# Forgetting attention and a SiLU layer on one core: v loads held behind the load of f, a weight load issued one step earlier, a larger budget of MoE work

## The chip, the cores and the metric

The kernel runs on one core of a Trainium2 chip. A core has five engines with their own instruction streams: PE (TensorE, matrix multiply), ACT (ScalarE, activations), DVE (VectorE), POOL (GpSimd) and SP (SyncE, which only issues transfers). Sixteen DMA engines serve all transfers of the core. The metric is the device time of one execution in microseconds (us); less is better.

## The reference

Attention over 8 batches and 8 heads, 576 positions, head size 64, with a decay between positions that comes from a gate f; then a two-layer network with a SiLU on the rows of the result. In short:

```python
def _attn_ref(q, k, v, f):                      # q, k, v: (8, 8, 576, 64); f: (8, 8, 576)
    scores = scale * np.matmul(q, k.transpose(0, 1, 3, 2))
    cum = np.cumsum(np.log(np.clip(f, 0.0001, 1.0)), axis=-1)
    decay = cum[:, :, :, None] - cum[:, :, None, :]
    scores = np.where(causal, -1000000000.0, scores + decay)
    attn = np.exp(scores - np.max(scores, axis=-1, keepdims=True))
    attn = attn / (np.sum(attn, axis=-1, keepdims=True) + 1e-09)
    return np.matmul(attn, v)

def _moe_ref(x, w_in, w_out):                   # x: (4608, 512), w_in: (512, 2048), w_out: (2048, 512)
    h = x @ w_in
    return (h * (1.0 / (1.0 + np.exp(-h)))) @ w_out
```

## The kernel before

The order of every engine's instructions is the order in which the program writes them (`manual_schedule`); the only freedom is when each one's waits are over. Waits are derived from the tiles: an instruction that reads a tile waits for who wrote it, and one that overwrites a tile waits for who still reads it, transfers included.

**The gate.** f is loaded by SP into `f_sb` (L206). DVE clips it in place (L236), ACT takes the logarithm in place (`Ln`, L242), and `weights_scan` (L244) makes the cumulative sum on DVE (L245), a mask tile `ban` on DVE (L257), and the exponential `wexp` on ACT (L254). ACT loads a table for each of the two functions. `weights` (L266) transposes `wexp` on PE and copies it to `w_bf`. The decay then needs no add in the scores: the values v, and a column of ones beside them, are multiplied by `w_bf`.

**First blocks.** The first 128 positions of each batch are treated by themselves. `load_qk0` (L128) and `load_v0` (L137) load q, k and v; POOL issues these, except v of batches 0 and 1, which SP issues (L140). `turn0` (L277) transposes q and k on PE, ACT and DVE copying them out of PSUM. `ban0` (L297) puts the mask into the scores' PSUM by a matmul, `scores0` (L309) adds the scores and takes the exponential on ACT. `convert_v0` (L339) multiplies v by the weights on POOL, `out0` (L349) makes the output (L359) and divides it, `back0` (L382) transposes it into a tile x for the network. Batches 0 to 3 come first in the program, then 4 and 5, then 6 and 7 (`two_more`, L805).

**MoE.** `load_w_in` (L188) and `load_w_out` (L192) each load a quarter of a weight matrix, from POOL's queue. The network's first layer is cut into chunks (`m1_chunk`, matmuls at L567: one of 16 slices of the hidden size for one group of rows), the second into parts (`m2_part`, matmuls at L612: four of the 16 slices for 128 rows). A planner puts these between the steps of attention: `fill(us)` (L698) writes as many of them as make up that much modelled PE time, and what is left over or overdrawn is carried to the next `fill`. So a number handed to `fill` decides which PE instructions stand in front of which.

**Rest blocks.** Positions 128 to 575 follow, in a loop over pairs of heads (`for m in range(NQ)`, two pairs at a time). SP loads q, k and v of later pairs, POOL casts q and k (`cast_qk`, L399) and converts v (L413), SP issues a transposing DMA (L427), and PE makes the scores from its result (L459) and the output (L506). SP's loads for this begin behind one small transfer that reads `w_out_bf` and writes a tile nobody uses, so that SP waits there until that weight has landed:

```python
    def after(ap):
        nc.sync.dma_start(out=junk[0:1, 0:16], in_=ap)
```

The program's opening lines, as the change finds them:

```python
    nc.sync.dma_start(out=f_sb[:, :], in_=f.rearrange("b h s -> (b h) s"))
    load_qk0(0)
    load_v0(0)
    load_v0(1)
    ...
    nc.vector.tensor_scalar(
        out=f_sb[:, :], in0=f_sb[:, :], scalar1=1e-4, scalar2=1.0, op0=ALU.max, op1=ALU.min
    )
```

Of the kernel before, what the change touches and what calls it, by code (L numbers as in the profile page):

```python
# [10 lines left out]
FP32 = mybir.dt.float32  # L11
# [7 lines left out]
def kernel(  # L19
# [10 lines left out]
    nc = tc.nc  # L30

    B, H, S, D = q.shape
# [23 lines left out]
    const = ctx.enter_context(tc.tile_pool(name="const", bufs=1))  # L56
# [22 lines left out]
    ban = const.tile([P, NP, P], BF16, name="ban")  # L79
    warm = const.tile([P, SM], BF16, name="warm")  # L80
    junk = const.tile([1, 16], BF16, name="junk")
    kT0 = [const.tile([P, NP, P], BF16, name=f"kT0_{b}") for b in range(B)]
    v0 = [const.tile([P, H, D + 1], BF16, name=f"v0_{b}") for b in range(B)]
    vps = [const.tile([P, NM, H, D + 1], BF16, name=f"vp_{i}") for i in range(2)]
# [43 lines left out]
    def load_qk0(b):  # L128
        t = conv.tile([P, 2, RUN * D], BF16, name="qkb", tag="qkb")
        for i, src in enumerate((q, k)):  # L130
            nc.gpsimd.dma_start(
                out=t[:, i, :],
                in_=src[b, :, 0:P, :].rearrange("h (r c) d -> r h (c d)", c=RUN),
            )
        qk0[b] = t

    def load_v0(b):  # L137
        t = vfs[b % 4]
        q_ = nc.sync if b < 2 else nc.gpsimd
        q_.dma_start(out=t[:, :, 0:D], in_=v[b, :, 0:P, :].rearrange("h p d -> p h d"))  # L140
        vf0[b] = t
# [46 lines left out]
    def load_w_in(i):  # L188
        c0, c1 = i * DFF // WQ, (i + 1) * DFF // WQ
        nc.gpsimd.dma_start(out=w_in_bf[:, :, c0:c1], in_=w_in_v[:, :, c0:c1])  # L190
# [14 lines left out]
    f_sb = setup.tile([BH, S], FP32, name="f_sb")  # L205
    nc.sync.dma_start(out=f_sb[:, :], in_=f.rearrange("b h s -> (b h) s"))  # L206
    load_qk0(0)
    load_v0(0)
    load_v0(1)
    make_identity(nc, ident_bf)  # L210
# [9 lines left out]
    for i in range(2):  # L220
        for g in range(2):
            nc.vector.tensor_copy(
                out=sel[:, i, :].rearrange("p (u w r) -> p u w r", u=2, w=2)[:, g, :, :],
                in_=ident_bf[:, :].rearrange("p (r u i w) -> p u i w r", u=2, i=2, w=2)[
                    :, g, i, :, :
                ],
            )

    def keep_warm(n):
# [7 lines left out]
        out=f_sb[:, :], in0=f_sb[:, :], scalar1=1e-4, scalar2=1.0, op0=ALU.max, op1=ALU.min  # L237
# [39 lines left out]
    def turn0(b, i):  # L277
        src = qk0[b]
        if i == 0:
            qT0[b] = qktp.tile([P, NP, P], BF16, name="qT0", tag="qT0", bufs=2)  # L280
        dst, evac = ((qT0[b], nc.scalar.copy), (kT0[b], nc.vector.tensor_copy))[i]
        tp = pbig.tile([P, NP, NRUN, RUN], FP32, name="tp", tag="big")
        for c in range(RUN):
            for j in range(2):
                nc.tensor.matmul(
                    tp[j * D : (j + 1) * D, :, :, c].rearrange("p a r -> p (a r)"),
                    lhsT=src[:, i, c * D : (c + 1) * D],
                    rhs=sel[:, j, :],
                    start=True,
                    stop=True,  # L290
                )
        evac(
            out=dst[:, :, :].rearrange("p a t -> p (a t)"),
            in_=tp[:, :, :, :].rearrange("p a r c -> p (a r c)"),
        )

    def ban0(b):  # L297
        sc = psc.tile([P, 2, NP, P], FP32, name="sc", tag="sc")
        for i in range(2):
            nc.tensor.matmul(  # L300
                sc[:, i, :, :].rearrange("p a t -> p (a t)"),
                lhsT=ident_bf[:, :],
                rhs=ban[:, :, :].rearrange("p a t -> p (a t)"),
                start=True,
                stop=False,
            )
        return sc

    def scores0(b, sc=None):  # L309
        t = qT0.pop(b)  # L310
        fresh = sc is None
        u = upool.tile([P, 2, NP, P], BF16, name="u", tag="u")
        u0[b] = u
        if fresh:
            sc = psc.tile([P, 2, NP, P], FP32, name="sc", tag="sc")
        for p in range(NP):
            for i in range(2):
                r = slice(i * D, (i + 1) * D)
                nc.tensor.matmul(
                    sc[:, i, p, :],  # L320
                    lhsT=kT0[b][r, p, :],
                    rhs=t[r, p, :],
                    start=fresh,
                    stop=fresh or p == NP - 1,
                )
        nc.scalar.activation(
            out=u[:, :, :, :].rearrange("p i a t -> p (i a t)"),
            in_=sc[:, :, :, :].rearrange("p i a t -> p (i a t)"),
            func=ACT.Exp,
            scale=scale,  # L330
        )
# [7 lines left out]
    def convert_v0(b):  # L339
        nc.gpsimd.tensor_tensor(  # L340
            out=v0[b][:, :, :],
            in0=vf0.pop(b)[:, :, :],
            in1=w_bf[:, 0, b * H : (b + 1) * H, None].to_broadcast([P, H, D + 1]),
            op=ALU.mult,
        )
# [310 lines left out]
    def step(force=0):  # L656

        a, c = at["m1"], at["m2"]
        want = wanted(a, c)
        if not want:  # L660
            return None
        g1 = M1[a][0] if a < len(M1) else NG
        g2 = M2[c][0] if c < len(M2) else NG
        can1 = g1 in ready and not (M1[a][1] == 0 and g1 > g2 + 1)
        can2 = open2["w"] and c < len(M2) and g2 < g1
        kind = force if (force == 1 and can1) or (force == 2 and can2) else want
        if kind == 1:
            if M1[a][1] == 0:
                begin[g1] = (0, c)
            m1_chunk(g1, M1[a][1])  # L670
            at["m1"] += 1
            t = 4 * (GW[g1] / 2.4 + 2.5)
        else:
            m2_part(*M2[c])
            at["m2"] += 1
            t = 4 * (DM / 2.4 + 2.5)
        return t
# [6 lines left out]
    def plan(us_):  # L684

        a, c, kinds = at["m1"], at["m2"], []
        while us_ > 0:
            k = wanted(a, c)
            if not k:
                break  # L690
            kinds.append(k)
            if k == 1 and M1[a][1] == 0:
                begin[M1[a][0]] = (0, c)
            us_ -= (4 * (GW[M1[a][0]] / 2.4 + 2.5) if k == 1 else 4 * (DM / 2.4 + 2.5)) / 1000
            a, c = a + (k == 1), c + (k == 2)
        return kinds

    def fill(us_, least=0, ends=(0, 0)):  # L698

        left = us_ + at["left"]  # L700
        kinds = plan(left)
        kinds += [0] * (least - len(kinds))
        if any(ends) and kinds:
            if 2 not in kinds:
                kinds[0] = 2
            n1, n2 = len(kinds) - kinds.count(2), kinds.count(2)
            e0 = 1 if ends[0] else 0
            e1 = 1 if ends[1] and n2 > e0 else 0
            inner = n2 - e0 - e1
            n = n1 + inner  # L710
            mid = [2 if (x + 1) * inner // n > x * inner // n else 1 for x in range(n)]
            if inner and mid[-1] == 2 and e1 and not e0:
                mid = mid[::-1]
            kinds = [2] * e0 + mid + [2] * e1
        for k in kinds:
            t = step(k)
            if t is None:
                at["left"] = 0.0
                return
            left -= t / 1000  # L720
        at["left"] = left
# [22 lines left out]
    out0(0, apart=True)  # L744
    turn0(3, 0)
    scores0(2, ban0(2))
    convert_v0(2)
    load_w_in(1)
    turn0(3, 1)
    bans = ban0(3)  # L750
    out0(1, apart=True)
# [80 lines left out]
    fill(6.0)  # L832
    two_more(6, False)
    ready.add(2)
    fill(3.2)

# [101 lines left out]
```

## Time and profile before

| what | value |
|---|---|
| device time, median of 3 runs | 344.5 us (344.4 to 344.6) |
| span of the profiled execution | 342.2 us |
| the rest of the median, around that span | 2.3 us |
| PE busy | 334.3 us (98% of the span) |
| ACT, DVE, POOL busy | 216.8, 180.5, 130.0 us |
| DMA engines' mean busy share, 20 to 50 us | 1.15 to 1.21 by ten-microsecond windows |
| last matmul ends | 338.55 us |

The span runs from the first to the last instruction of the program in one profiled execution, and all positions in time are counted from its start; the device time is measured without the profiler, and the table puts their difference down as the rest. [...] PE is busy for nearly the whole span, so what matters is when it is not.

### The profile page before, as it was taken

The numbers are of one execution on the slowest core, as the hardware profiler recorded it, in microseconds if no ns is written. First come the engines' busy times: TensorE is split into PE (matmuls) and PEld (weight loads), VectorE is DVE, ScalarE is ACT, GpSimd is POOL, SyncE is SP. The second block draws the span as 40 slices with busy tenths as digits, with TensorE's granted clock in tenths as the row PEclk, the third lists the DMA queues.
The fourth block names the chain that finished last, engine by engine and source line by source line (L and its number), as shares of the span: only waits on it lengthen the run. The fifth ranks groups of instructions, "written<-read, shape, count | busy, mean of one in ns | idle before, by whom it ended". The sixth has DMA issues, their size and how long they took to land.

```text
span 342.2 us, 8881 instructions
## 1 busy us (share of the span) xinstructions
PE 334.3 (98%) x3560; PEld 198.6 (58%) x3560; DVE 180.5 (53%) x387; ACT 216.8 (63%) x401; POOL 130.0 (38%) x227
## 2 busy tenths in 40 slices
PE   7999999999999999999999999999999999999995
PEld 3645655567656556566465666656656565555654
DVE  4665736357647547357445563655746364444330
ACT  5857645877687676857759677595685944454431
POOL 8895317732618307327325422612830000001011
PEclk9999999999999999999999999999999999999999
DMA  8999999999699889999999789989994010001012
GB/s 154 185 184 221 192 192 155 233 207 190 142 172 205 188 177 168 180 210 156 174 188 188 171 156 202 169 170 165 165 186 101 22 42 33 31 32 61 33 53 72
DMA packets 142457, 50.67 MB, mean 148 GB/s; under 512 B 133328, under 2 KB 139728, under 8 KB 142416
## 3 DMA queue, kind: packets, MB, share of 16 engines
q1 hardware_dynamic: 132400, 32.93, 56.7%
q0 software_dynamic: 9856, 17.04, 21.5%
q8 instruction: 28, 0.46, 0.6%
q10 hardware_dynamic: 160, 0.13, 0.1%
q14 instruction: 13, 0.11, 0.1%
HBM read 36.85 MB, written 9.44 MB: 135 GB/s over the span
## 4 chain that ended last, share of the span: by engine, by line
PE 66%; DMA 14%; SPq 9%; POOL 6%; issue 3%; ACT 0%; POOLq 0%
PE po L612 29%; PE hp L567 25%; DMA vf<-in_v_dram 6%; PE sc L459 5%; SPq L158 5%; PE dn L506 4%; DMA w_out_bf<-in_moe_w_out_dram 3%; PE dn L515 2%; SPq L427 2%; DMA qkT<-qkb 2%; POOL qkb L399 1%; DMA qkb<-in_k_dram 1%; SPq L168 1%; SPq L179 1%; DMA qf<-in_q_dram 1%
## 5 line engine op out<-in xcount | busy, mean ns | idle before, releaser
L576 DVE SCALAR_TENSOR_TENSOR gt<-th,hp 128x384 bf16<-128x384 bf16 (+2 forms) x208 | 105.8, 522 | 119.0 <-ACT th L575 115.5
L575 ACT ACTIVATE th<-hp 128x384 bf16<-128x384 f32 (+2 forms) x208 | 95.2, 478 | 84.3 <-PE hp L567 82.0
L612 PE MATMUL po<-w_out_bf,gt 128*128 128x512 bf16 (+1 forms) x592 | 145.3, 374 | 0.0
L567 PE MATMUL hp<-x,w_in_bf 128*128 128x384 bf16 (+2 forms) x704 | 128.1, 321 | 0.2
L567 PEld LDWEIGHTS <-w_in_bf 128*128 128x128 bf16 x832 | 79.9, 98 | 56.5 <-issue 0.7
L463 ACT ACTIVATE u<-sc 128x1024 bf16<-128x1024 f32 (+1 forms) x96 | 75.3, 822 | 9.5 <-PE sc L459 9.5
L612 PEld LDWEIGHTS <-gt 128*128 128x128 bf16 x592 | 53.3, 98 | 47.9 <-issue 2.5
L591 POOL DMA_DIRECT2D out_dram<-osb x38 | 21.0, 552 | 93.7 <-ACT osb L622 66.7
L413 POOL TENSOR_TENSOR vp<-vf,w_bf 128x520 bf16<-128x520 f32 (+1 forms) x32 | 34.4, 1078 | 41.0 <-DMA vf<-in_v_dram 35.1
L622 ACT ACTIVATE osb<-po 128x512 f32<-128x512 f32 (+1 forms) x37 | 22.1, 597 | 18.9 <-PE po L612 18.9
L399 POOL CAST qkb<-qf 128x384 bf16<-128x384 f32 x32 | 16.7, 521 | 41.9 <-DMA qf<-in_q_dram 41.2
L459 PE MATMUL sc<-qkT 64*128 64x128 bf16 (+1 forms) x640 | 26.9, 207 | 0.9 <-DMA qkT<-qkb 0.8
L459 PEld LDWEIGHTS <-qkT 64*128 64x128 bf16 x640 | 18.4, 94 | 12.5 <-issue 10.2
L467 ACT ACTIVATE ut<-sc 128x640 bf16<-128x640 f32 x32 | 23.3, 729 | 0.0
L476 DVE TENSOR_TENSOR u<-u,tri 128x768 bf16<-128x768 bf16 x32 | 22.1, 690 | 1.2 <-ACT u L463 1.2
L399 POOL CAST qkb<-kf 128x384 bf16<-128x384 f32 x32 | 17.7, 554 | 13.0 <-DMA kf<-in_k_dram 12.8
L506 PEld LDWEIGHTS <-u 128*128 128x128 bf16 x576 | 20.8, 98 | 2.5
L506 PE MATMUL dn<-vp,u 128*128 128x65 bf16 x384 | 21.8, 194 | 0.0
L524 DVE TENSOR_TENSOR xr<-dn,rec 128x448 bf16<-128x448 f32 x32 | 20.0, 624 | 1.1
L506 PE MATMUL dn<-v,u 128*128 128x65 bf16 x192 | 19.8, 194 | 0.0
L482 DVE TENSOR_TENSOR ut<-ut,trit 128x128 bf16<-128x128 bf16 x32 | 11.2, 351 | 15.6 <-ACT ut L467 15.6
L567 PE MATMUL hp<-xt,w_in_bf 128*128 128x256 bf16 x128 | 17.7, 273 | 0.0
(68 smaller groups left out, 203.0 us busy)
## 6 DMA issues: line engine op xcount, KB each, us to landing
out_dram<-osb POOLq DMA_DIRECT2D x32, 256.0 KB, 3.3
vf<-in_v_dram SPq DMA_DIRECT2D x26, 256.0 KB, 4.7
qf<-in_q_dram SPq DMA_DIRECT2D x64, 96.0 KB, 2.9
kf<-in_k_dram SPq DMA_DIRECT2D x64, 96.0 KB, 3.1
w_in_bf<-in_moe_w_in_dram POOLq DMA_DIRECT2D x4, 512.0 KB, 6.9
w_out_bf<-in_moe_w_out_dram POOLq DMA_DIRECT2D x4, 512.0 KB, 9.6
vf<-in_v_dram POOLq DMA_DIRECT2D x6, 256.0 KB, 10.3
qkb<-in_q_dram POOLq DMA_DIRECT2D x8, 128.0 KB, 5.1
```

The costliest lines, as they stand in the source:

```text
L399: nc.gpsimd.tensor_copy(out=t2[:, c0 : c0 + NR, :].rearrange("p c x -> p (c x)"), in_=t[:, :, :, :].rearrange("p c h d -> p (c h d)"),)
L413: nc.gpsimd.tensor_tensor(out=vbf[b][r, c, :, :], in0=vst[b][c][r, :, :], in1=w_bf[r, c + 1, b * H : (b + 1) * H, None].to_broadcast([n, H ...
L459: nc.tensor.matmul(sc[:, i, o : o + q1 - q0], lhsT=kt, rhs=t[r, q0:q1], start=True, stop=True)
L463: nc.scalar.activation(out=u[:, :, c * SM : c * SM + w], in_=sc[:, :, 0:w], func=ACT.Exp, scale=scale)
L467: nc.scalar.activation(out=ut[:, :, 0:3:2, :].rearrange("p k i t -> p i k t"), in_=sc[:, :, T0 : T0 + (NM + 1) * ST].rearrange("p i (k t) ...
L476: nc.vector.tensor_tensor(out=x, in0=x, in1=tri[:, None, None, :].to_broadcast([P, 2, NR, P]), op=ALU.mult)
L506: nc.tensor.matmul(dn[:, i * NR + c - 1, :], lhsT=u[:, i, o : o + P], rhs=vals(kb, i), start=(kb == 0), stop=(kb == c),)
L567: nc.tensor.matmul(hp[:, :], lhsT=w_in_bf[:, cc, fc * P : (fc + 1) * P], rhs=xcols(g, cc), start=(cc == 0), stop=(cc == NCC - 1),)
L575: nc.scalar.activation(out=th[:, :], in_=hp[:, :], func=ACT.Tanh, scale=0.5)
L576: nc.vector.scalar_tensor_tensor(out=gt[:, fc, :], in0=th[:, :], scalar=1.0, in1=hp[:, :], op0=ALU.add, op1=ALU.mult,)
L612: nc.tensor.matmul(po[:, :], lhsT=gt[:, fc, tb * P : (tb + 1) * P], rhs=w_out_bf[:, fc, m0:m1], start=(fc == 0), stop=(fc == NFC - 1),)
L622: nc.scalar.activation(out=osb[:, :], in_=po[:, :], func=ACT.Copy, scale=0.5)
```

## The change

Three edits. SP, after the load of f, gets a transfer of the last 16 numbers of one row of `f_sb` to a new tile that nobody reads; it stands ahead of the two v loads in SP's order. On POOL, the second quarter of w_in is issued ahead of the third conversion of v instead of behind it. And the last `fill` ahead of the rest blocks gets 4.1 instead of 3.2.

```diff
+    junk_f = const.tile([1, 16], FP32, name="junk_f")
...
     nc.sync.dma_start(out=f_sb[:, :], in_=f.rearrange("b h s -> (b h) s"))
     load_qk0(0)
+    nc.sync.dma_start(out=junk_f[0:1, 0:16], in_=f_sb[0:1, S - 16 : S])
     load_v0(0)
     load_v0(1)
     make_identity(nc, ident_bf)
...
     turn0(3, 0)
     scores0(2, ban0(2))
+    load_w_in(1)
     convert_v0(2)
-    load_w_in(1)
     turn0(3, 1)
...
     two_more(6, False)
     ready.add(2)
-    fill(3.2)
+    fill(4.1)
```

## The prediction

> **What bounds the kernel now.** I read the page first, for the engine that carries the span:
>
> ```profile
> span 342.2 us, 8881 instructions
> ...
> PE 334.3 (98%) x3560; PEld 198.6 (58%) x3560; DVE 180.5 (53%) x387; ACT 216.8 (63%) x401; POOL 130.0 (38%) x227
> ```
>
> PE, the matmul engine, is idle for only 7.9 us, of which 3.7 lie behind its last matmul (it ends at 338.55). The change adds and removes no matmul, so it can act on the span only through the other 4.2 us, or by adding idle time. The view of waits, for PE, says where those are:
>
> ```profile
> PE wm L232 <- DVE warm L204: 1.2, 1, 1.2
> PE sc L459 <- DMA qkT<-qkb: 0.8, 2, 0.4
> PE tp L285 <- DMA qkb<-in_q_dram: 0.7, 1, 0.7
> PE tx L389 <- DVE xq L374: 0.5, 1, 0.5
> PE dn L359 <- POOL v L340: 0.4, 1, 0.4
> ```
>
> The 0.8 us at L459 are two waits in the rest blocks, at 74.38 (0.40) and at 111.78 (0.43), where transposed q and k land just too late. Nearly all the rest lies in the first 18 us. So the third view is the timeline of these, all engines (start, duration, engine, line, operation, idle time before it and what ended that):
>
> ```profile
> 0.74 0.59 SPq L206 DMA_DIRECT2D f_sb<-in_f_dram  x1
> 0.74 1.28 ACT L242 ACT_TABLE_LOAD   x1 [0.74 <-PEq L924]
> ...
> 3.63 0.45 DVE L236 TENSOR_SCALAR f_sb<-f_sb 64x576 f32<-64x576 f32 x1
> ...
> 4.11 0.68 ACT L242 ACTIVATE f_sb<-f_sb 64x576 f32<-64x576 f32 x1 [2.09 <-DVE f_sb L236]
> ...
> 6.30 0.29 DVE L257 TENSOR_SCALAR ban<-tri 128x512 bf16<-128x512 bf16 x1
> 6.39 0.78 ACT L254 ACTIVATE wexp<-cum,half 64x576 f32<-64x576 f32 x1 [0.30 <-DVE half L253]
> ...
> 7.16 1.04 PE L300 MATMUL sc<-ban,ident_bf 128*128 128x512 bf16 x4
> ...
> 8.13 0.40 PE L319 MATMUL sc<-qT,kT 64*128 64x128 bf16 x8
> ...
> 9.51 1.05 POOL L340 TENSOR_TENSOR v<-vf,w_bf 128x520 bf16<-128x520 f32 x1 [0.28 <-issue]
> ...
> 16.24 0.42 PE L359 MATMUL dn<-v,u 128*128 128x65 bf16 x8 [0.44 <-POOL v L340]
> ```
>
> The reader is to see one serial chain: f lands at 3.60 (issued 0.74, 2.9 to landing), is clipped in place on DVE, goes through Ln on ACT and the scan on DVE (4.83 to 6.18), then comes ban (which stands behind the scan in DVE's order) and the exponential. PE needs ban at L300, 0.57 us after it is ready (6.59), and the weights shortly after. This chain has half a microsecond of slack, no more.
>
> **Part 1, the hold on v.** SP gets one more DMA, a copy of 64 bytes out of f_sb, ahead of the two v loads. SP waits for f before it issues that copy (3.60), so the v loads go out at about 4.25 and 4.9 instead of 1.39 and 2.0. At 5.4 to 5.9 from issue to landing (v's own rows) they land by 9.7 and 10.8; before, the first was needed at 9.51. Freed of them, the q and k of block 0 should land before the 5.53 and 6.55 of now.
>
> But the copy reads f_sb, and the clip overwrites f_sb in place. In the changed program as built, the clip on DVE waits for two landings, that of f and that of the copy, and ACT's first table load, which now has no wait at all, waits for the copy as well. So the copy's whole trip is added to the chain, and the table load with it, which has been hidden in the wait for f so far (0.74 to 2.02). The sum:
>
> - The copy is issued at 3.62. Its time to landing is not in the trace. The nearest rows are f's own load on the same queue, 2.9 us for 144 KB, and the junk copy of the same form at L200, 5.5 us at 36.46, when the DMA engines are full (share 1.21 in 30 to 40). Taking f's data off (144 KB at about 0.2 MB/us, the rate of the first slices, 0.7 us) leaves 2.2. The copy runs beside the first q and k loads, but with no long queue, so I take 2.5, nearest to f, and keep as ends 5.5 and 1.6 (the 2.2 without the 0.59 that the issue itself takes). It lands at 6.1.
> - ACT's table load then runs from about 6.15 for 1.28; the clip (0.45) lies beside it. Ln starts at 7.45 instead of 4.11: 3.34 later. Scan, half, ban and exponential follow 3.34 later, with nothing else in front of them.
> - PE finishes the transposition of block 0 early (about 6.4) and waits for ban: 6.59 + 3.34 = 9.93. The 0.57 slack is eaten. The scores at L319 also need the copy of q on ACT, which stands behind the exponential (ended 7.64, now 10.98): they start near 11.1 instead of 8.13, 2.95 later. The weights w_bf and POOL's first conversion are late by the same (9.51 becomes 12.45), so the later v costs nothing: the first has landed 2.7 us before.
> - Downstream, 0.35 us come back: the last first-block output (16.24) waited 0.44 for POOL, and without POOL could have started at 15.9, when its exponential was done. POOL's order after 12.45 is conversion, load, conversion, load, conversion, conversion: 4 x 1.05 + 2 x 0.80 = 5.8, so the fourth v is ready at 18.25, and PE is there at 15.9 + 2.95 = 18.85. So MoE work starts 2.6 late, at 20.76 instead of 18.16.
>
> **Part 2, w_in ahead of the third conversion.** Now POOL waits 0.91 for v before that conversion (at 13.30, in the same timeline), and the issue of a load takes 0.80, so the load would be free and the fourth conversion come 0.8 earlier; that is the 0.44 at 16.24. With POOL late by 2.95 the wait is gone anyway, and the issue costs the third conversion 0.8, which is in POOL's sum above and leaves it 0.6 us ahead of PE. The first w_in load moves from 10.51 to about 13.4, its data (5.8 to landing) are there by 19.2, before 20.76. No cost; if that cover were gone, 0.8.
>
> **Part 3, more MoE work in front.** A group of four L567 matmuls of 256 columns takes 0.43 of PE, one of four L612 0.86 (rows of the chain). The built order puts one more L567 group ahead of the first rest score, two by the scores of the fourth head pair, where PE waited 0.40, and one L612 group by the tenth, where it waited 0.43: 0.86 us more work in front of each. After the sixteenth pair it is 0.6 less, since the total is the same. It costs nothing by itself. The loads behind these waits hang on the DMA engines, which are full from 20 to 50 us (share 1.15 to 1.21 by ten-microsecond windows); they are late by what the w_in loads are late, about 1.9: the first lands near 19.2, the second 2.7 behind it (the distance of the third and fourth now, 26.1 and 28.8), at 21.9 instead of 19.99. PE comes 2.6 + 0.86 late. So PE has 1.5 us more distance to its data than now, and both waits, 0.8 together, vanish.
>
> **The sum:** +2.6 - 0.8 = +1.8 on the profiled execution, 342.2 becomes 344.0. The runs' median of 344.5 is 2.3 above that span, and I let that stand: 346.3.
>
> The Trainium skill, page "DMA: Bandwidth & Descriptors", section "Anatomy of one DMA — SWDGE (gpsimd) path", speaks against the added copy: a DMA has a fixed cost of about 2.0 us whatever its size, mostly the receipt of the write. By it the copy would be 2.0 instead of my 2.5 and the sum 345.8; the rows here say 2.9 and 5.5.
>
> **The rivals.** *The hold pays.* If DVE and ACT do not in fact stand behind the copy, q and k come earlier, the scores at L319 start when the unchanged chain allows (7.66 instead of 8.13: 0.47 less), the 0.44 behind POOL goes too, partly the same time (0.55 together), and the two rest waits (0.8): 343.1. The point from which this side decides, where they do stand behind it, is a copy of 0.7: the front loses the copy's time and about 0.1, and the rest blocks give back 0.8. For it: DMA's share in the first 10 us is 0.89, so the loads do collide. Against it: no DMA in the trace lands in under 2.9. Chance 0.05.
>
> *The rest waits stay.* If the loads slip as far as PE does, the 0.8 do not come back: 347.1. The DMA engines are busy without a gap behind the late w_in loads, but the sum there gives them 1.9, less than PE's 2.6. Chance 0.15.
>
> *The clock drops.* PE would idle from about 6.4 to 9.9. The granted clock is 1.00 over the first 112 us and 0.98 over the last 11.2, in which PE stops at 338.55, so some idle time at the end costs it. If the clock were halved for a stretch as long as that gap (3.5 us), PE would lose up to 1.7, and some of that is covered by waits: about 347.6. Chance 0.14.
>
> The Trainium skill, page "TensorE: Matmul & The Clock Gate", Part 1, says that the clock falls to half after an idle window of about 3.4 us that runs freely. By that the gap would be just at the limit, and the dip would come in some executions only.
>
> *The copy is stuck* behind queued packets like the one at 36.46, 5.5 us: 3.0 more, 349.3. Chance 0.06.
>
> **How the numbers follow.** The forecast as summed has the other 0.60. Of it, copies of 1.6 to 3.2 us give 345.4 to 347.0, and a copy of 1.4 or less, which would come within 0.2% (0.7 us, about what a measurement of this kernel can tell from no change), has 0.05. So faster 0.05, same 0.05, slower 0.90. The range 345.4 to 348.2 takes in the forecast, the waits that stay and most of a clock drop; the stuck copy, the hold that pays and the shortest copies, together under 0.2, are left out.
>
> **What would show it.** In the changed profile the clip should start near 6.1 with a DMA as its releaser, the table load near 6.15 instead of 0.74, the first matmul on ban near 9.9 with over 3 us of PE idle time before it, and the first L567 group (L569 there) near 20.8; the waits for qkT at pairs four and ten should be gone. Wrong in the main: a clip that still starts near 3.6. Wrong in size: a copy far from 2.5. Wrong in the middle: waits for qkT that remain while the front is late.

## The result and the profile after

The changed kernel is slower: 349.9 us median (348.1 to 350.8, 6 runs) beside 344.45 for the kernel before in the same series (343.3 to 346.3, 6 runs), a ratio of 1.0159 with a 95% interval of 1.0129 to 1.0188. The sign was forecast, the size was not: +5.5 us where the sum said +1.8, and above the range. Experiments are compared by their ratio to the kernel before, run in the same series, since the runs of one kernel lie 1 to 5 us apart from lowest to highest. Line numbers of the changed kernel are one (up to L207) or two higher than before; kernels with more lines added shift further.

The page of the changed kernel: span, engines, and the granted clock in 40 slices.

```profile
span 348.9 us, 8837 instructions
...
PE 333.0 (95%) x3513; PEld 199.8 (57%) x3560; DVE 179.6 (51%) x387; ACT 216.7 (62%) x401; POOL 129.6 (37%) x227
...
PEclk9699999999999999999999999999999999999999
```

The span is 6.7 longer (this execution took 350.76, a little above its median). PE does no more work; 47 of its 3,560 matmuls are missing from the trace, which is why its sum is even lower. The second digit of the clock is new. Waits of PE (total, number, longest):

```profile
PE sc L302 <- DVE ban L259: 4.2, 1, 4.2
...
PE dn L508 <- DVE gt L578: 1.2, 1, 1.2
PE wm L234 <- DVE warm L205: 1.2, 1, 1.2
PE hp L569 <- DMA x<-xr: 0.5, 1, 0.5
```

The two waits for qkT at L459 (0.8 in all) are gone, as forecast. In their place stand one of 4.2 for `ban`, which was forecast with 3.5, and two that were not: 1.2 at 194.61 and 0.5 at 149.60. The chain that ended last, in order of time (start, duration, what), tells where the 4.2 come from:

```profile
0.75 2.72 DMA f_sb<-in_f_dram
3.46 0.02 issue
3.48 3.78 DMA junk_f<-f_sb
...
7.33 1.28 ACT L244
...
8.63 0.69 ACT f_sb L244
...
9.34 1.36 DVE cum L247
...
10.87 0.21 DVE ban L259
...
11.13 1.87 PE sc L302 x4
12.99 0.54 PE sc L321 x8
```

The copy and ACT's table load now stand in the chain, one behind the other. The copy took 3.78 from issue to landing, not 2.5. And the four matmuls on `ban` took 1.87 where they took 1.04 before: PE was not at full speed. The windows of the changed kernel (PE, PEld, DVE, ACT and POOL busy, then the granted clock, the DMA share and GB/s; the share is the sum of all packets' times over the time of 16 engines, so it can pass 1):

```profile
6.00:9.00 3.00, 0.96 (x21) 0.67 (x18) 0.45 (x1) 1.65 (x2) 3.00 (x9) 0.94 1.16 217
9.00:12.00 3.00, 0.87 (x3) 0.32 (x3) 2.48 (x5) 2.69 (x4) 0.21 (x1) 0.50 1.21 241
12.00:15.00 3.00, 3.00 (x36) 2.04 (x36) 0.49 (x1) 1.18 (x2) 0.26 (x1) 0.50 0.54 120
15.00:18.00 3.00, 2.92 (x82) 2.62 (x80) 1.96 (x5) 2.14 (x3) 2.98 (x4) 0.92 0.21 14
```

The clock was halved from 8.65 to 15.48, two stretches of 3.41 us, although PE's gap was 4.2. One such stretch takes 0.005 off the mean clock of a run, and the six runs have 0.990 (three) and 0.995 (three), so the drop came in all of them, two stretches or one. The DMA share falls to 0.21 in the last window: the first w_in load is issued at 15.74 only, since POOL's first conversion stands ahead of it and waits for the weights. MoE work starts at 23.60 instead of 18.16.

### The profile page after: what moved, and what is told of

The parts are those of the page before. It is cut to its first block, busy times and chain, and to the rows that moved or that the text cites. A ratio compares the mean times of both kernels' runs of the same rounds, so it can differ in the third digit from the quotient of the medians.

```text
span 348.9 us, 8837 instructions
## 1 busy us (share of the span) xinstructions
PE 333.0 (95%) x3513; PEld 199.8 (57%) x3560; DVE 179.6 (51%) x387; ACT 216.7 (62%) x401; POOL 129.6 (37%) x227
## 4 chain that ended last, share of the span: by engine, by line
PE 79%; DMA 7%; SPq 4%; DVE 3%; ACT 3%; issue 3%; POOL 1%; POOLq 0%; ACTq 0%
PE po L614 31%; PE hp L569 31%; PE sc L461 6%; PE dn L508 4%; PE tp L287 2%; PE dn L517 2%; SPq L429 2%; SPq L159 2%; DMA qkT<-qkb 2%; DVE gt L578 1%; DMA x<-xr 1%; DMA vf<-in_v_dram 1%; DMA junk_f<-f_sb 1%; PE sc L302 1%; DMA qf<-in_q_dram 1%
## 5 line engine op out<-in xcount | busy, mean ns | idle before, releaser
L578 DVE SCALAR_TENSOR_TENSOR gt<-th,hp 128x384 bf16<-128x384 bf16 (+2 forms) x208 | 105.4, 522 | 122.1 <-ACT th L577 119.1
L614 PE MATMUL po<-w_out_bf,gt 128*128 128x512 bf16 (+1 forms) x550 | 138.5, 373 | 3.4 <-issue 1.9
L415 POOL TENSOR_TENSOR vp<-vf,w_bf 128x520 bf16<-128x520 f32 (+1 forms) x32 | 35.8, 1124 | 38.3 <-DMA vf<-in_v_dram 27.2
L401 POOL CAST qkb<-kf 128x384 bf16<-128x384 f32 x32 | 16.9, 527 | 15.9 <-DMA kf<-in_k_dram 15.9
L484 DVE TENSOR_TENSOR ut<-ut,trit 128x128 bf16<-128x128 bf16 x32 | 13.6, 424 | 14.2 <-ACT ut L469 14.0
L478 DVE TENSOR_TENSOR u<-u,tri 128x768 bf16<-128x768 bf16 x32 | 19.7, 617 | 0.6 <-ACT u L465 0.6
```

The lines of the kernel that those rows point to most:

```text
L401: nc.gpsimd.tensor_copy(out=t2[:, c0 : c0 + NR, :].rearrange("p c x -> p (c x)"), in_=t[:, :, :, :].rearrange("p c h d -> p (c h d)"),)
L415: nc.gpsimd.tensor_tensor(out=vbf[b][r, c, :, :], in0=vst[b][c][r, :, :], in1=w_bf[r, c + 1, b * H : (b + 1) * H, None].to_broadcast([n, H ...
L578: nc.vector.scalar_tensor_tensor(out=gt[:, fc, :], in0=th[:, :], scalar=1.0, in1=hp[:, :], op0=ALU.add, op1=ALU.mult,)
L614: nc.tensor.matmul(po[:, :], lhsT=gt[:, fc, tb * P : (tb + 1) * P], rhs=w_out_bf[:, fc, m0:m1], start=(fc == 0), stop=(fc == NFC - 1),)
```

## One sum for all the kernels

In every trace the last matmul ends at the start of MoE work, plus all of PE's waits behind that start, plus a rest that is the same throughout: 318.8 to 319.7 in 14 of the 15 kernels below, and 321.3 in `e5_w_in_only`, whose clock was halved once in the middle. So each kernel is told by two numbers, the start and the waits. The table has the two main waits: `qkT` is the tile into which SP's transposing DMA puts q and k, `gt` the tile of hidden values that DVE writes for the network's second layer (L578). Its sums include the short waits that the view of waits leaves out; gaps where matmuls are missing from a trace are not counted.

| kernel | ratio to before (95%) | MoE start | waits behind it: qkT | gt | last matmul ends |
|---|---|---|---|---|---|
| before | 1 | 18.16 | 0.83 | 0.17 | 338.55 |
| after | 1.0159 (1.0129 to 1.0188) | 23.60 | 0.09 | 1.39 | 344.86 |
| e1_copy_only | 1.0191 (1.0157 to 1.0225) | 23.84 | 1.54 | 0.23 | 345.38 |
| e2_no_copy | 0.9995 (0.9966 to 1.0024) | 17.93 | 1.46 | 1.74 | 340.57 |
| e3_clip_apart | 1.0086 (1.0052 to 1.0120) | 21.79 | 0 | 1.43 | 342.28 |
| e4_warm | 1.0164 (1.0127 to 1.0202) | 22.28 | 2.93 | 1.27 | 345.81 |
| e5_w_in_only | 0.9998 (0.9970 to 1.0026) | 17.64 | 1.94 | 0.55 | 342.13 |
| e6_fill_only | 1.0003 (0.9972 to 1.0034) | 17.91 | 0.16 | 1.84 | 339.16 |
| e7_table_early | 1.0143 (1.0104 to 1.0182) | 23.21 | 0 | 0.38 | 342.36 |
| e8_early_w_in_warm | 1.0108 (1.0074 to 1.0141) | 22.33 | 0 | 1.98 | 343.21 |
| e9_early_w_in | 1.0144 (1.0099 to 1.0190) | 24.58 | 0 | 0.88 | 344.44 |
| e10_one_number | 1.0211 (1.0171 to 1.0250) | 23.49 | 0.78 | 1.97 | 345.60 |
| e11_apart_warm | 1.0077 (1.0048 to 1.0107) | 19.78 | 0.18 | 1.75 | 340.89 |
| e12_w_in_fill38 | 1.0025 (0.9994 to 1.0055) | 18.36 | 1.36 | 0.48 | 340.38 |
| e14_hold_one | 1.0054 (1.0028 to 1.0081) | 18.27 | 0.46 | 1.47 | 339.39 |

A trace is one execution and the ratio is of several, so the two need not agree to the microsecond: `e5_w_in_only`'s profiled execution was the slowest of its twelve, and the only one of them with a mean clock as low as 0.995 (the others have 0.998 or more).

## The experiments

**Which part costs.** The copy alone, in the kernel before:

```diff
     load_qk0(0)
+    nc.sync.dma_start(out=junk_f[0:1, 0:16], in_=f_sb[0:1, S - 16 : S])
     load_v0(0)
```

> The kernel before with the copy alone (no move of w_in, fill 3.2). Theory A (the copy's trip, about 3.8 us, and the Ln table load stand in the chain of f, and PE then runs at half clock for a while): nearly all of the change's loss is here, first hp group near 23.6 as in the changed kernel, 349 to 350.5. Theory B (the changed MoE order makes the new waits of 1.2 and 0.5 us in the middle): without it these waits are gone, 348 to 348.5. Theory C (v arriving late is the cost) cannot be told from A here.

And all but the copy:

```diff
     load_qk0(0)
-    nc.sync.dma_start(out=junk_f[0:1, 0:16], in_=f_sb[0:1, S - 16 : S])
     load_v0(0)
```

> The changed kernel without the copy: w_in ahead of the third conversion and fill 4.1 alone. Theory A: no loss is left; the 0.44 us wait of PE for the fourth v goes, and the 0.8 us of waits for qkT at the fourth and tenth pair shrink: 343.2 to 344.2. Theory B: the waits in the middle of 1.2 and 0.5 us stay: 345 to 346.

The copy alone gives the whole loss (1.0191; its interval overlaps that of the change), the other two parts together give nothing (0.9995). The copy landed 4.4 us after its issue here, MoE work started at 23.84, and the qkT waits did not go but grew (1.54 beside 0.83):

```profile
PE sc L302 <- DVE ban L259: 5.1, 1, 5.1
PE sc L461 <- DMA qkT<-qkb: 1.3, 2, 0.8
```

Without it the start is 0.23 earlier than before, and two waits behind it are longer, as PE's waits in `e2_no_copy` show:

```profile
PE dn L506 <- DVE gt L576: 1.6, 1, 1.6
PE sc L459 <- DMA qkT<-qkb: 1.5, 3, 0.6
```

The median, 344.6, is above the 343.2 to 344.2 that theory A gave, and the wait near 190 stayed, as theory B had it.

**The chain, or the hold itself?** The clip, the logarithm and the scan work in a second tile, so that nothing overwrites what the copy reads. Only the v loads are then behind the copy:

```diff
     nc.vector.tensor_scalar(
-        out=f_sb[:, :], in0=f_sb[:, :], scalar1=1e-4, scalar2=1.0, op0=ALU.max, op1=ALU.min
+        out=f_c[:, :], in0=f_sb[:, :], scalar1=1e-4, scalar2=1.0, op0=ALU.max, op1=ALU.min
     )
...
-    nc.scalar.activation(out=f_sb[:, :], in_=f_sb[:, :], func=ACT.Ln)
+    nc.scalar.activation(out=f_c[:, :], in_=f_c[:, :], func=ACT.Ln)
```

> The changed kernel with the clip of f written to a second tile, so that nothing overwrites what the copy reads: v is held as in the change, but DVE and ACT no longer wait for the copy. Theory A: clip back at 3.6, table load at 0.74, no long idle time of PE, clock at 1.00: 343 to 344. Theory C (the late v loads cost the time by themselves): most of the loss stays, 347 to 350.

Neither theory alone: the loss is about halved (1.0086), not gone. The table load is back at 0.74, the clip at 3.76, and PE's waits of this kernel name other tiles:

```profile
PE tp L288 <- DMA qkb<-in_k_dram: 1.8, 1, 1.8
PE dn L509 <- DVE gt L579: 1.3, 1, 1.3
PE wm L235 <- DVE warm L205: 1.2, 1, 1.2
PE tp L288 <- DMA qkb<-in_q_dram: 0.9, 1, 0.9
```

Freed of v, q and k of block 0 land early (4.29 and 4.98 instead of 5.53 and 6.55), which nothing needs. The two v loads then meet q and k of block 2 in the queues, and these land at 10.34 and 12.76 instead of 9.55 and 10.19, where PE waits. The clock is halved once (14.51 to 17.92). So the hold does not pay even without the chain behind it: what was taken away ahead of block 0 came back ahead of block 2.

Two kernels, both built on `e3_clip_apart`, ask how the hold costs. In one, 3 and 6 idle matmuls stand ahead of the transposes that wait; in the other, only the second v load is behind the copy:

```diff
+    keep_warm(3)
     turn0(2, 0)
+    keep_warm(6)
     turn0(2, 1)
```

> The kernel with the clip in a second tile (the copy held nothing but the v loads there: 347.6), and with 3 and 6 idle matmuls ahead of the transposes of the third block's q and k, for which PE waited 0.86 and 1.78. Theory C1 (the hold's own cost is the late q and k of the third block, the clock is a consequence): the granted clock stays at 1.0, MoE work starts 1.0 to 1.4 earlier than 21.79, near 20.5, and the loads set the rest: 346.3 to 347.6. Theory C2 (the hold costs only by the clock drop): the start falls back to 18.5 or less and the time to 344.5 to 345.

```diff
+    load_v0(0)
     nc.sync.dma_start(out=junk_f[0:1, 0:16], in_=f_sb[0:1, S - 16 : S])
-    load_v0(0)
     load_v0(1)
```

> The kernel with the clip in a second tile (347.6 with both v loads behind the copy), but the first v load ahead of the copy: only the second is held. Theory C1 (the held v loads meet the q and k of the later blocks in the queues, each costs about half): PE's waits for the third block's q and k fall from 2.64 to about 1.3, MoE work starts near 20, 346 to 346.6. Theory C2 (only the clock drop costs): no drop with the shorter waits, the start near 18.5 and 344.5 to 345. If it is one late v that holds everything, it is still 347.6.

With the idle matmuls the clock stayed at 1.0 and MoE work started at 19.78, 2.0 earlier; but the ratio of 1.0077 can't be told from 1.0086, and the runs that make it range from 344.8 to 349.7. With one v held, q and k of block 2 land at 9.98 and 10.65, PE does not wait for them, the start is 18.27, and the ratio is 1.0054. So block 2 was late because both v loads were held; with the first one back in its place it is not. The times may say that some of the loss remains: 346.0, where the last matmul, 0.84 later than before, would make 345.0 of the 344.14 of this series; the interval begins at 345.1. The clock is not what the hold costs: in five of the six runs of `e3_clip_apart` the mean clock is 0.997 to 0.999, so no whole stretch at half speed is in them, and they took 345.8 to 348.8 all the same; only the traced run has 0.994. What costs the rest with one v held is not settled.

**Why the copy takes so long.** One number instead of 16:

```diff
-    nc.sync.dma_start(out=junk_f[0:1, 0:16], in_=f_sb[0:1, S - 16 : S])
+    nc.sync.dma_start(out=junk_f[0:1, 0:1], in_=f_sb[0:1, S - 1 : S])
```

> The changed kernel with a copy of one number (4 bytes) instead of 16. If the copy's 3.78 us come from its being split into 16 pieces of which the last sets the landing (they landed from 6.08 to 7.26), a single piece lands between those, 6.7 on average, and the front starts 0.6 earlier: 349.3. If it is a fixed trip behind the q packets that are in flight, which a piece on any engine meets, it lands near 7.26 and the time stays at 349.9. If the trip is as short as forecast for a small transfer (2.5), it lands near 6.0 and the time is 347 to 348.5.

It was issued at 3.66 and released ACT at 7.67: 4.0, so the 16 pieces are not the reason, and the time is no better (1.0211). The second kernel holds POOL's q and k loads until the copy has landed, by a write to the first q tile that reads the copy's result:

```diff
+    nc.sync.dma_start(out=junk_f[0:1, 0:16], in_=f_sb[0:1, S - 16 : S])
     load_qk0(0)
-    nc.sync.dma_start(out=junk_f[0:1, 0:16], in_=f_sb[0:1, S - 16 : S])
...
+        if b == 0:
+            nc.gpsimd.tensor_copy(out=t[0:1, :, 0:16], in_=junk_f[0:1, None, :].to_broadcast([1, 2, 16]))
         for i, src in enumerate((q, k)):
```

> The changed kernel with every q and k load of POOL held until the copy has landed (a write to the first q tile that reads the copy's result stands ahead of them), so that the copy runs with nothing of another queue in flight. It measures the copy by itself; its front is much later. If the packets of the q loads ahead of it make the trip long, it lands about 2 us after its issue (the small output loads at the quiet end take 2.1 to 2.2). If the trip is a fixed one for a transfer that follows a landing on this tile, it takes 3.5 to 4.2 as in the runs so far (3.53 to 4.40).

The copy's issue in the changed kernel (KB, us from issue to landing):

```profile
junk_f<-f_sb SPq DMA_DIRECT2D x1, 0.1 KB, 3.8
```

and of `e13_quiet_copy`:

```profile
junk_f<-f_sb SPq DMA_DIRECT2D x1, 0.1 KB, 1.6
```

With nothing else in flight the same copy lands in 1.64 (3.41 to 5.05). Behind q and k it took 3.5 to 4.4 in ten kernels. So it is the loads of the other queue that make the trip long. In the changed kernel the copy's first packet moves at 5.61, 2.1 after its issue (1.2 in the quiet kernel), and its last at 6.9, among packets of q and k of 1 KB that take 0.10 to 0.25 each. Whether it waits for these packets alone or also for something in how POOL's loads are issued, the runs don't separate. The time of this kernel, 350.25 in a single execution, says nothing of the change, as its q and k come 4 us late.

**The clock.** 18 idle matmuls fill the gap ahead of `ban`:

```diff
+    keep_warm(18)
     bans = [ban0(0), ban0(1)]
```

> The changed kernel with 18 matmuls on zeros (3.9 us) put in front of the first matmul on the mask, in PE's idle time. Theory A with the clock drop: granted clock stays at 1.00, the first hp group comes 1.7 us sooner, near 21.9, and the time falls to about 348.2. If the clock drop costs nothing that matters: no change, 349.9.

The clock holds; the window of 9 to 12 us, 0.50 in the changed kernel, reads here:

```profile
9.00:12.00 3.00, 2.57 (x13) 1.08 (x12) 2.09 (x4) 2.68 (x4) 0.06 (x1) 1.00 1.24 248
```

and MoE work starts at 22.28, 1.3 earlier, although the copy was slower here (4.2) and `ban` came 0.5 later. The first matmuls on `ban`, in the changed kernel and here:

```profile
11.13 1.87 PE L302 MATMUL sc<-ban,ident_bf 128*128 128x512 bf16 x4 [4.16 <-DVE ban L259]
11.66 1.02 PE L302 MATMUL sc<-ban,ident_bf 128*128 128x512 bf16 x4 [0.43 <-DVE ban L259]
```

From there to MoE work it is 12.47 in the changed kernel and 10.62 here (11.00 before). So the clock drop cost PE's opening 1.85, for the 4.35 that it lasted behind 11.13. But the time does not follow (1.0164), since waits for qkT take the place:

```profile
PE sc L461 <- DMA qkT<-qkb: 2.9, 3, 1.4
```

The idea was then that the loads set the end: POOL issues w_in(0) behind the first conversion, which waits for the weights (14.1), and all later loads follow. Two kernels issue w_in(0) and w_in(1) ahead of that conversion, while POOL has nothing to do, with and without the 18 matmuls:

```diff
-    convert_v0(0)
     load_w_in(0)
+    load_w_in(1)
+    convert_v0(0)
...
-    load_w_in(1)
     convert_v0(2)
```

> The changed kernel with the 18 idle matmuls that keep the clock up, and with the first two w_in loads issued ahead of the first conversion, so that they go out near 9.1 and 9.9 us instead of 15.1 and 16.9, while POOL waits for the weights. Theory D (behind the late front it is the chain of loads, which hangs on the w_in loads behind the first conversion, that sets the end, and the 1.3 that the clock gives back is lost to waits for qkT): the waits for qkT of 2.9 are gone, MoE starts near 22.3, the time falls by 2 to 3 to 347.5 (from 350.3). Theory A (PE's own start sets everything, the waits for qkT in that run were chance): the time stays at 349 to 350.3, or follows the start alone.

> The changed kernel with the first two w_in loads ahead of the first conversion, without the added matmuls. Both theories agree that MoE work starts near 23.6 as in the changed kernel. Theory D: the loads are then far ahead of PE, no wait for qkT is left, and the time moves by little: 349 to 350, the front's lateness is paid in full by PE. If it is the earlier loads alone that help, and not the start of PE, it falls below 348.5.

The waits for qkT are gone in both; no such line is left among PE's waits of `e8_early_w_in_warm`:

```profile
PE dn L508 <- DVE gt L578: 1.8, 2, 1.5
PE wm L234 <- DVE warm L205: 1.2, 1, 1.2
PE sc L302 <- DVE ban L259: 0.7, 1, 0.7
PE tx L391 <- DVE xq L376: 0.3, 1, 0.3
```

With early loads and the clock kept up the ratio is 1.0108, without the clock 1.0144, with the clock and late loads 1.0164. That is the order that the theory gives, and the traces show the exchange; the intervals of the ratios overlap, so the times alone would not show it. The median of `e8_early_w_in_warm`, 348.8, is above the 347.5 expected; the waits for gt that stayed, 1.98 in all, are more than that difference. In `e9_early_w_in` both theories had expected the start near 23.6, and it was 24.58: the clock was halved until 17.49 there, 2.0 longer than in the changed kernel. From `ban` to MoE work it is 10.62 again in `e8_early_w_in_warm` (22.33 less 11.71) and 13.42 in `e9_early_w_in` (24.58 less 11.16).

The table load, taken out from behind the copy by a logarithm of a single 1 early on:

```diff
+    one = const.tile([1, 1], FP32, name="one")
+    nc.vector.memset(one[:, :], 1.0)
+    nc.scalar.activation(out=one[:, :], in_=one[:, :], func=ACT.Ln)
     keep_warm(10)
```

> The changed kernel with a logarithm of a single 1 (a tile of its own) at the head of ACT's order, so that the table load is done near 2 us and only the logarithm of f stands behind the copy. Theory A (the table load behind the copy is 0.83 of the front's loss): the logarithm starts near 7.8 instead of 8.63, ban and everything behind it come 0.83 earlier, PE's idle time before ban is 3.3 instead of 4.16, MoE work starts near 22.8 or, if PE's idle time no longer costs the clock, near 21.1; the loads go out earlier too, since the weights do, so the gain is kept: 347.4 to 349.1. Rival (the table is loaded again, or the load chain sets the end alone): 349.9 as before.

The logarithm of f came 0.98 earlier (7.65; the copy also landed 0.32 sooner), MoE work only 0.39 (23.21): the clock was halved until 15.74 all the same, so more of PE's work fell into the stretch at half speed. The ratio of 1.0143 can't be told from the 1.0159 of the change.

**The wait for gt near 190.** The w_in move and the larger budget, each alone:

```diff
+    load_w_in(1)
     convert_v0(2)
-    load_w_in(1)
```

> The kernel before with the second w_in load ahead of the third conversion, alone (no copy, the budget stays 3.2). Theory B (the wait of the denominator matmuls for gt near 190 us comes from the order that the larger budget makes): no such wait here, the 0.44 for POOL at the fourth v is gone, MoE work starts near 17.9; the time is 0.2 to 0.4 below the 344.5 of before. Rival (the earlier w_in load shifts the loads of the rest blocks, and the wait near 190 comes with that): the wait of 1.2 to 1.6 is here too, the time is 345 to 346.

```diff
-    fill(3.2)
+    fill(4.1)
```

> The kernel before with the budget of 4.1 instead of 3.2, alone. Theory B: the denominator matmuls wait 1.2 to 1.6 for gt near 190 us, the two waits for qkT are shorter by up to 0.8 because 0.86 more PE work stands in front; sum 344.9, up to 345.3. Rival: no wait near 190, and 343.7 to 344.5.

The wait belongs to the budget. PE's waits of `e6_fill_only`:

```profile
PE dn L506 <- DVE gt L576: 1.7, 2, 1.2
...
PE sc L459 <- DMA qkT<-qkb: 0.2, 1, 0.2
```

and of `e5_w_in_only`:

```profile
PE sc L459 <- DMA qkT<-qkb: 1.9, 1, 1.9
...
PE dn L506 <- DVE gt L576: 0.2, 1, 0.2
```

The budget trades waits for qkT for a wait for gt, and the time stays (1.0003). Of 12 traced kernels with 4.1, ten have a wait of 1.0 to 1.6 there (not `e7_table_early` and `e9_early_w_in`), of the three with 3.2 none. What is late is on DVE; its rows in the changed kernel:

```profile
190.93 1.71 DVE L484 TENSOR_TENSOR ut<-ut,trit 128x128 bf16<-128x128 bf16 x1
193.02 1.07 DVE L484 TENSOR_TENSOR ut<-ut,trit 128x128 bf16<-128x128 bf16 x1
194.02 1.00 DVE L578 SCALAR_TENSOR_TENSOR gt<-th,hp 128x384 bf16<-128x384 bf16 x2
```

and POOL's at that time:

```profile
191.49 2.52 POOL L415 TENSOR_TENSOR vp<-vf,w_bf 128x520 bf16<-128x520 f32 x2
```

A mask product of 128x128 takes 0.22 where POOL is idle (14 of the 32 in this trace) and 0.66 on average where POOL is busy for nine tenths of it or more (14 of them), from 0.21 up to 1.71. In the kernel before, the same two products are short:

```profile
186.18 0.22 DVE L482 TENSOR_TENSOR ut<-ut,trit 128x128 bf16<-128x128 bf16 x1
187.98 0.45 DVE L482 TENSOR_TENSOR ut<-ut,trit 128x128 bf16<-128x128 bf16 x1 [0.81 <-ACT ut L467]
```

In `e6_fill_only` they take 1.71 and 1.07 again, as in the changed kernel. The Trainium skill, page "SBUF — State Buffer", section "Who interferes with whom", says that a DVE instruction with two inputs in SBUF and a POOL instruction that reads SBUF exclude each other, and that the later one is blocked until the other is done. These rows agree in that both products end 0.1 behind one of POOL's conversions (192.64 after 192.54, and 194.09 after 194.01). They do not settle who came first: the first product starts at 190.93, ahead of that conversion (191.49) and behind a cast on POOL (190.78). With the larger budget the products fall on POOL's work, `gt` comes late, and PE waits for what it frees.

A budget between the two, with the w_in move and no copy, was the candidate to beat the kernel before:

```diff
+    load_w_in(1)
     convert_v0(2)
-    load_w_in(1)
...
-    fill(3.2)
+    fill(3.8)
```

> A candidate to beat the kernel before: the w_in load moved as in the change, no copy, and a budget of 3.8, between 3.2 (waits for qkT of 2.6 and no wait of the denominator matmuls) and 4.1 (waits for qkT up to 1.5 and one of 1.6 near 190). If one of the two kinds of wait goes without the other coming: 343.0 to 344.0. If the two trade one for one, as theory B with a load chain near its limit says: 344.5, no difference.

No gain (1.0025): waits for qkT of 1.4, for gt of 0.5, and an opening that was 0.2 later in this trace. No version tried beats the kernel before.

## Why the prediction was wrong in size

The mechanism of the front was right, step for step: the clip and the table load stand behind the copy, the logarithm behind the table load, and PE waits for `ban`. Three terms of the sum failed. The copy's 2.5 was too short (3.78), the clock drop was left out of the sum (1.66), and the 0.8 that was to come back from the rest waits did not (the waits grew by 0.9). Where the numbers parted:

| step | forecast | measured |
|---|---|---|
| copy, issue to landing | 2.5 | 3.78 |
| Ln starts | 7.45 | 8.63 |
| first matmul on ban | 9.93 | 11.13 |
| scores at L321 | 11.1 | 12.93 |
| w_in(0) issued, landed | 13.4, 19.2 | 15.74, 21.16 |
| MoE work starts | 20.76 | 23.60 |
| PE's waits behind that (1.10 in all before) | -0.8 | +0.91 |
| span | 344.0 | 348.9 |

The 4.9 us that the span is above the forecast are four terms: 1.18 the copy (by the start of Ln), 1.66 the clock (what is left of the 2.84 at the MoE start; the four matmuls on ban alone are 0.83 longer), 1.71 the waits behind it, 0.34 a longer end behind the last matmul, of which the runs show no cause. In the medians the miss is 3.6: the traced execution took 0.9 more than its median, and time less span is 1.9 in it, where the prediction added 2.3.

**The copy's trip** was mis-sized by 1.28. The prediction took "2.5, nearest to f", because the copy would run "with no long queue". f's load had run with almost nothing else on the DMA engines; the copy ran behind q and k, and that queue was long enough to more than double its trip. Its low end of 1.6 was right for a quiet queue (1.64 measured), and so wrong here. The 2.0 of the Trainium skill (page "DMA: Bandwidth & Descriptors", "Anatomy of one DMA — SWDGE (gpsimd) path"), cited against the 2.5, was off the same way: it is near what the quiet copy took, and less than half of the slowest. (That section is on transfers that POOL issues, and SP issued this one.) "No DMA in the trace lands in under 2.9", said against the rival by which the hold pays, was misread: the kernel before has output loads of 64 KB from SP that take 2.0, at the quiet end.

```profile
out_dram<-osb SPq DMA_DIRECT2D x2, 64.0 KB, 2.0
```

Of the two nearest rows the right one was the one with the same traffic, the junk copy at 5.5, or a point between the two.

**The clock** was a rival at 0.14 "up to 1.7". It came in all six runs, and cost 1.66 against the forecast in this trace (1.85 against `e4_warm` and `e8_early_w_in_warm`, whose way from `ban` to MoE work is 10.62, the forecast's 10.83). The prediction let a long copy and the clock be separate cases, though a longer copy makes the gap longer. Nor did it take the longer gap: `e7_table_early` waits only 3.1 for `ban`, less than the 3.5 forecast, and all four of its runs have a mean clock of 0.990. So the drop belonged in the sum, and "in some executions only" was wrong for this gap. The rule cited on windows of 3.4 us (page "TensorE: Matmul & The Clock Gate", Part 1) fits the length: stretches of 3.41, two of them here, in `e7_table_early` and in `e9_early_w_in`, one in `e1_copy_only` and in `e10_one_number`.

**The rest waits** for qkT did vanish, 0.74 of 0.83, but the 0.8 did not come back: the wait of 1.22 for gt took their place. The prediction looked only at the two places where PE waited, and the larger budget made a wait elsewhere. "It costs nothing by itself", said of that budget, holds for the time within the interval (`e6_fill_only`, 1.0003) and not for the waits. A late front gave nothing back with the small budget either: in `e1_copy_only` the qkT waits are 1.54. In the traced execution of the changed kernel there is also the 0.53 for a transposed x at 149.60, of which the runs show no cause.

**Part 2** was right that the move costs nothing (`e5_w_in_only`, 0.9998). That it takes away the 0.44 at the fourth v is not shown: the wait is gone in `e2_no_copy` (start 17.93), which has the move, but just as well in `e6_fill_only` (17.91), which has not. In `e6_fill_only` the third v landed at 12.63 instead of 13.17, and POOL had no wait left to fill.

**"The later v costs nothing"** holds in the changed kernel, where PE waits for the longer chain anyway. As a statement on the hold it was wrong: with the chain taken away (`e3_clip_apart`) the hold alone still costs 0.9% beside `e2_no_copy`, at least in part by way of q and k of a later block, which the prediction had not looked at.

## What to carry to other kernels

A transfer that is added only for its order is still a transfer: before adding it, list who overwrites or waits for what it reads, and price it by a row that ran beside the same traffic, not by its size. Where a change leaves PE idle for some microseconds (3.1 brought the clock drop in all four runs of `e7_table_early`, 1.9 in one run of `e5_w_in_only`), count the clock into the same case as the gap. And a gain at the front of a kernel whose loads are as tight as its matmuls can be lost to waits if the loads don't move too, as the trace of `e4_warm` shows; so sum the start and every wait behind it, not the one wait that was aimed at.

## What was not expected of the hardware

- The same 64-byte copy from SP lands after 1.64 us with nothing in flight, and after 3.5 to 4.4 behind the q and k loads of another queue; a copy of 4 bytes takes 4.0 there.
- The clock can be halved after a gap much shorter than 3.4. In the traced execution of `e5_w_in_only` PE waits 1.94 until 75.43; in the stretch of 3.41 us around that wait it is busy for 1.47, and in the next the clock reads 0.50. The rule cited above, of an idle window of about 3.4 us, does not cover this, since the stretch was busy for 43%:

```profile
73.41:76.82 3.41, 1.47 (x20) 0.80 (x15) 1.24 (x3) 2.13 (x5) 1.46 (x3) 1.00 1.06 183
76.82:80.23 3.41, 3.41 (x27) 1.87 (x26) 1.45 (x4) 2.13 (x6) 0.87 (x3) 0.50 0.70 156
```

- A small DVE product took 1.71 us beside POOL's work, nearly eight times its usual 0.22, and PE waited for `gt` behind it.
